# Another fixed task list for a one-core kernel of chunked attention with memory and a SiLU feed-forward block

## The chip, the cores and the metric

The kernel runs on one core of one Trainium2 chip. The core has five engines that run side by side, each with its own instruction stream that it takes in order: TensorE (PE, matrix products; its weight loads are PEld), VectorE (DVE), ScalarE (ACT), GpSimd (POOL) and SyncE (SP, here only the issuer of DMAs). The metric is the device time of one run in microseconds. Before the change it is 305.55 us, the median of 3 runs (305.26 to 305.59).

## The reference

Input x has 2048 tokens of 640 features in bf16. There are 32 heads of 20 features, and the sequence is cut into 4 segments of 512 tokens. Cut to what matters:

```python
h  = x + A(layernorm(x))          # attention with memory
h2 = h + B(layernorm(h))          # B(y) = silu(y @ w1) @ w2, w1 is 640 x 1728

# A: q, k, v = x @ wq, x @ wk, x @ wv, per head and segment s
logits = q_s k_s^T * 20**-0.5 + causal mask
a_dot  = softmax(logits) @ v_s
a_mem  = phi(q_s) @ M / (phi(q_s) @ z + 1e-6)   # phi(t) = t+1 if t > 0 else exp(t)
o_s    = g * a_mem + (1 - g) * a_dot            # g = sigmoid(beta), per head
M += phi(k_s)^T @ v_s ;  z += sum over phi(k_s) # for the next segment
A = concat(o_s) @ wo
```

## The kernel before

Everything is cut into about 1490 **tasks**, each a few instructions on one engine, and a list written out in the code, `ORDER`, fixes their order. `Graph.schedule` walks the list: the name gives the task, what follows a slash gives its engine where it has a choice (A for ACT, D for DVE), and the numbers after a colon give the buffer slots it takes in its pools. `Tracker` then records reads and writes of every buffer slot and puts semaphore waits before the instructions that need them. So the list decides three things: the order on each engine, the engine of each task that can run on two, and the slots. In time the engines run freely against each other, held only by these waits. PSUM has eight banks of 512 f32 columns (pool `ps`), and a score task takes four of them.

The tasks, with the line that issues them in the kernel before. The first digit of a name is the segment:

- `x0` to `x12`, `w_...`, `beta`: loads (L567, L570, L579). x0, x1 and the weights go out on SP, x2 and x3 on ACT's queue. x4, x8 and x12 bring four blocks of 128 tokens each, the first four one block each.
- `zpad` (L583): a zeroed tile on DVE. `warm` (L585): an activation on ACT that reads it. `fillN` (L604): N matmuls of zpad by zpad, 256 columns each, into a free bank; nobody reads the result. `sel` (L618) builds an identity on DVE from POOL's `iota`.
- `n1_st`, `n1_ra`, `n1_rb`, `n1_ap` (L711 to L732): layer norm of a block: statistics on DVE, reciprocal root in two steps on POOL, application on DVE. For the first four blocks `n1_tp` (L741) transposes on PE against the identity and `n1_te` (L750) copies the result to xT on ACT. Later blocks go through `n1_tr`, a transposing DMA on SP (L756). `n2_...` is the same for the second layer norm, with hT as its target.
- `re_wq`, `re_wk` (L682 on ACT, L684 on DVE): wq and wk copied into a layout by groups of four heads.
- `v`, `ve` (L783, L793/L794): v of a block, and its copy to Vx. `pr`, `qe` (L817, L825/L826): one group column of q or k, and its copy to QK. `ex`, `pha`, `phb` (L832, L839, L845): phi of it. `vt` (L857): twelve small DMAs per segment on SP, which put the rest of q and k, features of the last 12 heads, into tile QKV.
- `qk` (L893), `e` (L904), `mk` (L915): scores of four heads into four banks, two exponentials on ACT of two banks each (1024 or 768 elements per partition) into tile PT, and the causal mask on POOL. Segment 0 is cut in two halves (x and y); from segment 1 on a group has parts a, b and a shared part e.
- `av`, `oe`, `tn`, `nm`, `ad` (L936, L949/L951, L965 and L969, L982 to L1002, L1010): PT times V, copy, transposition back to tokens together with the memory's part, division, and addition into otok.
- `kt`, `mz`, `ma`, `mb` (L1050 to L1094): the memory: a transposing DMA of phi(k), products with V, accumulation, masking with constants that `mt`, `mta`, `mtb`, `mm` and `mzc` (L643 to L657) build once on POOL.
- `ot`, `wo`, `rs` (L1111, L1119, L1127): transposing DMA, output projection, residual.
- `h1`, `th`, `s` (L1148/L1153, L1162, L1168): feed-forward: product with w1, tanh on ACT, and (tanh + 1) times the product on DVE into sT. Two buffers hold the tanh. In segment 0 each runs in two halves of 256 columns.
- `h2`, `o`, `out` (L1195, L1208, L1213): product of sT with w2 in four parts, residual, store. The last block is stored in three column parts.

Segments overlap: while segment s has its scores and exponentials, the list places the projections of segment s+1 and the feed-forward block of segment s-1 between them on PE.

Of the kernel before, what the change touches and what calls it, by code (L numbers as in the profile page):

```python
# [373 lines left out]
mk6x_256 w_w1_1 w_w1_4 ve10/D qk2ya0:4 mk7x_0 v13:0 e2ya2:5 n1_ra9 mk7x_256 mk1yb_256 e2ya0 tn0y:2 av7x:3 ve13/D n1_rb8
oe7x/A:0 qk2yb0:4 nm0y:1 tn7x:0 e2yb0:1 av6x:1 nm7x:2 tn5x:2 av1y:3 e2yb2 oe6x/D:1 nm5x:3 tn6x:0 oe1y/A:0 qk3ya0:4
mk2yb_0 nm6x:0 e3ya0:2 n1_rb10 ot1:0 mk2yb_256 pha011:0 phb011 e3ya2 tn1y:2 pr101:1 mz02:0 qe101/D:0 av2y:3 ot0 ma02/A:3
qk3yb0:4 oe2y/D:1 mz00:1 e3yb2:0 phb041 pr100:3 ma00/D:0 kt01:1 nm1y:1 e3yb0 tn2y:2 zf1 qe100/D qk4ya0:4 mk3yb_0 kt04:0
wo1:0 e4ya0:6 nm2y:2 mk3yb_256 mtb1 e4ya2 w_w2_2 av3y:3 rs1 w_w1_3 ex031:0 qk4yb0:4 oe3y/D:0 w_w1_2 wo0:0 e4yb2:5
n2_st1:5 w_w2_1 e4yb0 epsg1 tn3y:2 ex101:1 n2_ra1 rs0 mm5 qk5ya0:4 pr140:3 n2_rb1 mk4yb_0 n2_st0:2 e5ya2:0 e5ya0 pr121:0
n2_ap1:0 n2_ra0 nm3y:0 qe140/A:0 mt0 n2_rb0 n2_tr1:0 qk5yb0:4 pr141:1 mta0 e5yb2:3 n2_ap0:2 mk4yb_256 n2_tr0 e5yb0 mtb0  # L380
pha031:1 phb031 av4y:2 mm6 qk6ya0:4 mm4 qe121/D:0 ex140:2 mk5yb_0 pr111:3 e6ya2:6 mk5yb_256 e6ya0 pr120:0 qe111/D:0
qe141/D ex121:0 qk6yb0:4 pha101:2 av5y:3 e6yb0:4 oe4y/D:0 h1_0_7_0:1 qe120/D e6yb2 h1_0_0_0:2 oe5y/D:1 th0_7_0:1 mk6yb_0
mk6yb_256 qk7ya0:4 th0_0_0:0 s0_7_0:0 tn4y:0 h1_0_8_0:3 e7ya0:2 nm4y:3 mz01:1 s0_0_0 mz04:0 e7ya2 ma01/D:2 phb101 kt10:0
kt03:1 h1_0_3_0:2 ma04/D:1 tn5y:1 th0_8_0:1 qk7yb0:4 th0_3_0:0 s0_8_0 av6y:0 e7yb0:0 s0_3_0 h1_0_1_0:3 nm5y:1 e7yb2
h1_0_12_0:2 th0_1_0:1 mk7yb_0 qk8a0:4 th0_12_0:0 pr110:1 e8a2:1 s0_12_0 s0_1_0 mm0 mk7yb_256 e8a0 mzc0 h1_0_10_0:2
qe110/D av7y:3 th0_10_0:1 vt19:0 qk8e0:4 s0_10_0 pr130:1 e8e2:0 vt16 oe6y/D:1 w_w2_3 n1_ap10:2 oe7y/D:0 e8e0 h1_0_5_0:2
pha121:0 qe130/D:0 w_w2_0 h1_0_11_0:3 th0_5_0:1 mk8e_0 qk8b0:4 s0_5_0 th0_11_0:0 tn7y:0 h1_0_6_0:1 e8b0:6 nm7y:3 mz03:2
ma03/D:4 s0_11_0 e8b2 h1_0_2_0:0 pha100:0 n1_ap8:1 h1_0_13_0:2 pha120:0 th0_2_0:1 qk9a0:4 mk8b_0 th0_13_0:0 pr131:3
s0_13_0 e9a2:4 mk8a_0 s0_2_0 mk8b_384 e9a0 h1_0_4_0:0 qe131/D n1_tr8:0 mk8e_256 h1_0_9_0:2 pha141:2 th0_6_0:1 mm3
th0_4_0:0 qk9b0:4 s0_6_0 mzc4 mzc6 ex100:1 mk9a_0 vt17 av8:3 s0_4_0 th0_9_0:1 mzc3 pha110:0 e9b2:3 h2_0_0:0 mm2 phb100  # L390
phb121 s0_9_0 mm9 pha111:1 mtb2 vt18 vt110 mzc9 mm8 e9b0 mm11 h2_0_1 oe8/D:0 mzc5 n1_tr10 ex141:1 mk9b_0 mm10 qk10a0:4
tn6y:3 h2_0_2 e10a2:5 phb141 mm1 vt11 nm6y:0 mzc2 n1_rb9 h2_0_3 e10a0 vt13 mb01:0 mm7 vt111 mzc1 qk10b0:4 mk9b_384 o0
h2_1_0:2 e10b2:2 ot3 mb00:0 e10b0 tn8:0 h2_1_1 n1_tr11 ex120:0 mk10b_0 nm8:2,1 qk10e0:4 ex111:1 h2_1_2 vt15 mk10b_384
phb111 n1_ap9:0 e10e2:1 mk10a_0 vt14 av9:0 e10e0 phb120 ot2 h2_1_3 oe9/A:0 ex110:0 mk10e_0 mk10e_256 qk11a0:4 kt12:1 o1
wo3:0 e11a0:6 pha130:0 mb02:0 phb110 e11a2 vt10 av10:2 rs3 n1_tr9 ex131:0 qk11b0:4 mk11a_0 oe10/D:1 tn9:0 e11b0:2
nm9:1,0 vt12 wo2:2 e11b2 ex130:1 mk11b_0 qk12a0:4 rs2 v20:0 e12a2:4 n2_st2:7 mzc7 e12a0 mzc8 mk11b_384 av11:2 pha131:0
n2_st3:1 ve20/A:1 qk13a0:4 mz12:3 e13a0:2 e13a2 v21:0 ma12 kt11:1 n2_ra3 phb130 n2_rb3 mzc11 mz10:3 n2_ra2 mzc10 ve21/A
n2_rb2 qk12b0:4 ma10 n2_ap3:1 ad8:0 e12b0:6 tn10:0 n2_tr3 pr210:3 nm10:0,1 mk13a_0 e12b2 mb03:0 qe210/A:0 ad9 qk12e0:4
oe11/D:1 pr220:0 e12e0:0 phb131 mk12b_0 n2_ap2:2 kt13:0 e12e2 mk12b_384 pr231:1 pha140:0 mk12a_0 qe220/A:0 n2_tr2
mk12e_0 qk13b0:4 qe231/D:0 tn11:2 e13b2:5 pr200:0 mk12e_256 nm11:3,0 ad10 e13b0 av12:1 qe200/D:0 mk13b_0 qk14a0:4 v23:2  # L400
e14a2:1 phb140 mk13b_384 oe12/D:1 mb04:0 e14a0 av13:1 ve23/A qk14b0:4 mz13:0 e14b2:3 pr221:2 ma13 oe13/D:0 e14b0
h1_0_7_1:3 qe221/A mk14b_0 qk14e0:4 th0_7_1:1 tn13:0 s0_7_1 mk14a_0 pr211:2 nm13:3,1 mk14b_384 e14e0:0 e14e2 h1_0_8_1:3
qe211/D mk14e_0 qk15a0:4 th0_8_1:1 pr241:0 e15a0:4 s0_8_1 mk14e_256 ad11 e15a2 av14:2 qe241/D:0 ad13 mz11:1 oe14/A:0
qk15b0:4 ma11 mk15a_0 e15b0:1 tn14:2 h1_0_4_1:1 nm14:3,1 e15b2 pr201:0 th0_4_1:1 mk15b_0 tn12:4 s0_4_1 qe201/A
h1_0_12_1:7 nm12:0,0 mk15b_384 qk16b0:0 e16b0:2 th0_12_1:0 ad14 av15:6 h1_0_13_1:4 ad12 oe15/D:0 e16b2 pr240:5 pha200:0
s0_12_1 th0_13_1:1 pha210:0 pha211:0 tn15:6 s0_13_1 qe240/A ex210:0 qk16a0:0 nm15:0,0 pr230:4 e16a2:6 e16a0 h1_0_10_1:5
qe230/D ad15 h1_0_6_1:6 phb210 th0_10_1:1 mb10:0 ot6:0 qk16e0:0 th0_6_1:0 s0_10_1 h1_0_0_1:7 ex211:0 mk16b_0 s0_6_1
v22:4 e16e2:5 mk16b_384 ot7 th0_0_1:1 e16e0 s0_0_1 h1_0_5_1:6 vt210:0 h1_0_11_1:7 ve22/A mk16e_0 mk16a_0 ot4 qk17b0:0
th0_5_1:1 wo6:4 mk16e_256 e17b2:3 s0_5_1 phb211 out1 e17b0 ot5 av16:6 rs6 ex220:2 qk18b0:0 pha220:0 th0_11_1:0 wo7:4
vt23 kt21:0 phb220 e18b2:0 oe16/D:1 e18b0 s0_11_1 h1_0_9_1:6 rs7 h1_0_3_1:7 th0_9_1:1 n2_st6:6 ex221:1 qk17a0:0 vt21  # L410
wo4:4 th0_3_1:0 e17a0:6 s0_9_1 n2_ra6 kt14:1 mk17b_0 s0_3_1 e17a2 h1_0_1_1:6 rs4 vt28 vt22 h1_0_2_1:7 mb12:0 mk17b_384
th0_1_1:1 n2_st7:4 n2_rb6 qk18e0:0 vt211 th0_2_1:0 wo5:4 e18e2:1 s0_2_1 vt26 n2_ra7 mk17a_0 s0_1_1 e18e0 vt24 mb13:0
av17:6 rs5 n2_rb7 ex231:2 vt27 vt29 qk18a0:0 pha231:0 mk18e_0 ex200:0 n2_st5:0 vt20 e18a2:5 n2_st4:3 n2_ap7:0 h2_2_0:4
# [855 lines left out]
```

## Time and profile before

| | us |
|---|---|
| median of 3 runs | 305.55 |
| span of the profiled execution, first to last instruction | 303.6 |
| own time of that execution | not given beside its span; the median is 1.95 above the span |
| TensorE clock granted over the span | 1.00 |
| PE, chain of work that ended last | 72% of the span |
| ACT, same chain | 12% |
| DVE, same chain | 7% |
| exponentials (L904) on ACT | 156.3 busy, x168 |
| causal masks (L915) on POOL | 81.5 busy, x128 |
| h2 (L1195) and h1 (L1153) on PE | 64.8 and 62.5 busy |
| fillers (L604) on PE | 9.1 busy, x61 |

The profile is of one execution. An engine's busy time counts an instruction from its start to its end, also where it has to wait for something on the way; matmuls overlap, so the mean duration of one (about 300 ns for 320 columns) is longer than the spacing at which they follow each other. The chain of work that ended last is followed back from the last instruction, at each step to what released it. A stage table gives the busy time of every engine in a stretch of the span.

### The profile page before, as it was taken

What the parts mean: (1) busy time and instruction counts of PE and PEld (TensorE: products, weight loads), DVE (VectorE), ACT (ScalarE), POOL (GpSimd) and SP (SyncE); (2) the same over time, 40 slices, a digit from 0 to 9 for tenths busy, and PEclk for the clock granted to TensorE, in tenths of its full rate; (3) what the DMA queues carried; (4) which work ended last, traced back from release to release, by engine and by line L of the source; (5) the groups of instructions that cost most, each with busy time, mean ns of one, the idle gap of its engine ahead of it and who ended that gap; (6) DMA issues with size and microseconds to landing.
All of it is one profiled execution on the core that took longest, in us unless ns stands there. A gap on an engine that the chain in (4) does not pass through costs nothing.

```text
span 303.6 us, 7334 instructions
## 1 busy us (share of the span) xinstructions
PE 294.4 (97%) x2934; PEld 167.9 (55%) x2934; DVE 214.4 (71%) x492; ACT 226.6 (75%) x321; POOL 141.7 (47%) x280
## 2 busy tenths in 40 slices
...
GB/s 211 363 104 159 69 153 87 272 37 77 166 87 75 39 42 2 2 122 69 106 154 42 67 19 0 2 89 69 56 97 36 2 0 89 43 66 66 0 3 107
DMA packets 48721, 24.65 MB, mean 81 GB/s; under 512 B 39152, under 2 KB 47600, under 8 KB 48688
## 3 DMA queue, kind: packets, MB, share of 16 engines
...
q10 hardware_dynamic: 288, 0.33, 0.4%
...
## 4 chain that ended last, share of the span: by engine, by line
PE 72%; ACT 12%; DVE 7%; DMA 4%; SPq 2%; issue 1%; POOL 0%; ACTq 0%
PE ps_all L1195 17%; PE ps_all L1153 13%; PE ps_all L817 13%; ACT PT L904 8%; PE ps_all L893 7%; PE ps_all L1119 6%; PE ps_all L783 5%; PE ps_all L936 5%; DVE sT L1168 3%; DMA wv_sb<-in_A_wv_dram 2%; ACT th L1162 2%; PE ps_all L965 2%; PE ps_all L1058 2%; DMA x_tok<-in_A_x_dram 1%; PE ps_all L969 1%
## 5 line engine op out<-in xcount | busy, mean ns | idle before, releaser
L904 ACT ACTIVATE PT<-ps_all 128x1024 bf16<-128x1024 f32 (+1 forms) x168 | 156.3, 985 | 16.9 <-PE ps_all L893 15.9
L915 POOL TENSOR_SCALAR_AFFINE_SELECT PT<-PT 128x512 bf16<-128x512 bf16 x128 | 81.5, 650 | 52.8 <-ACT PT L904 51.5
L1195 PE MATMUL ps_all<-w_sb,sT 128*128 128x320 bf16 (+2 forms) x462 | 64.8, 295 | 0.1
L1153 PE MATMUL ps_all<-hT,w_sb 128*128 128x512 bf16 (+1 forms) x325 | 62.5, 337 | 0.5 <-DVE sT L1168 0.4
L1162 ACT ACTIVATE th<-ps_all 128x512 f32<-128x512 f32 (+2 forms) x70 | 34.0, 505 | 35.1 <-PE ps_all L1153 24.6
L1168 DVE SCALAR_TENSOR_TENSOR sT<-th,ps_all 128x512 bf16<-128x512 f32 (+2 forms) x70 | 37.6, 558 | 23.8 <-ACT th L1162 23.2
L1195 PEld LDWEIGHTS ps_all<-w_sb,sT 128*128 128x128 bf16 x462 | 43.2, 98 | 18.5 <-issue 1.9
L1153 PEld LDWEIGHTS ps_all<-hT,w_sb 128*128 128x128 bf16 x325 | 29.8, 98 | 25.4 <-issue 2.1
L1010 POOL TENSOR_TENSOR otok<-on 128x320 bf16<-128x320 bf16 x24 | 19.2, 804 | 23.7 <-DVE on L1002 23.6
L711 DVE BATCH_NORM_STATS2 stt<-x_tok 128x6 f32<-128x320 bf16 x64 | 27.8, 476 | 3.4 <-DMA x_tok<-in_A_x_dram 3.2
L1208 DVE SCALAR_TENSOR_TENSOR x_tok<-ps_all,x_tok 128x640 bf16<-128x640 f32 (+3 forms) x18 | 13.3, 748 | 19.0 <-PE ps_all L1195 18.9
L720 POOL TENSOR_TENSOR rst<-mvt,eps_c 128x1 f32<-128x1 f32 x32 | 7.1, 223 | 40.4 <-DVE mvt L714 36.0
L817 PE MATMUL ps_all<-xT,wqr 128*128 128x512 bf16 x100 | 25.0, 381 | 0.0
L783 PE MATMUL ps_all<-wv_sb,xT 128*128 128x320 bf16 x160 | 24.4, 300 | 0.4 <-DMA wv_sb<-in_A_wv_dram 0.3
L817 PE MATMUL ps_all<-xT,wkr 128*128 128x512 bf16 x100 | 24.8, 380 | 0.0
L1119 PE MATMUL ps_all<-wo_sb,oT 128*128 128x320 bf16 x160 | 24.1, 299 | 0.4 <-DVE rd L996 0.2
L936 PE MATMUL ps_all<-PT,Vx 128*32 128x256 bf16 (+3 forms) x576 | 24.4, 287 | 0.0
L893 PE MATMUL ps_all<-QK 20*128 20x256 bf16 (+3 forms) x360 | 20.5, 286 | 1.0 <-ACT PT L904 0.7
L1002 DVE TENSOR_TENSOR on<-ps_all,rd 128x640 bf16<-128x640 f32 x24 | 19.8, 824 | 1.9 <-POOL otok L1010 1.1
L826 DVE CAST QK<-ps_all 128x512 bf16<-128x512 f32 x25 | 16.9, 684 | 5.1 <-PE ps_all L817 5.0
L1119 PEld LDWEIGHTS ps_all<-wo_sb,oT 128*128 128x128 bf16 x160 | 14.8, 97 | 8.1 <-issue 2.8
L783 PEld LDWEIGHTS ps_all<-wv_sb,xT 128*128 128x128 bf16 x160 | 14.7, 98 | 7.9 <-issue 1.5
...
## 6 DMA issues: line engine op xcount, KB each, us to landing
...
```

Of the source, the lines that this page charges most:

```text
L711: T.add(DV, lambda e, hh=hh: e.bn_stats(out=stt[:, s, 6 * hh:6 * hh + 6], in_=xb[:, 320 * hh:320 * hh + 320]), reads=R((xa, xsub)), writes ...
L783: fns.append(lambda e, c=c, hh=hh: e.matmul(bank(ps, hh)[:, 0:320], lhsT=xT[:, c, 128 * i:128 * i + 128], rhs=wv_sb[:, c, 320 * hh:320 * h ...
L817: fns = [lambda e, kc=kc: e.matmul(bank(ps)[:, lo:hi], lhsT=wt[:, kc, c, :], rhs=xT[:, kc, lo:hi], start=(kc == 0), stop=(kc == NC - 1)) f ...
L893: fns.append(lambda e, j=j, o=o, r=r, q0=q0, q1=q1, qa=qa, ka=ka: e.matmul(ps_all[:, o:o + q1 - q0], lhsT=ka[32 * r:32 * r + DH, 128 * j:1 ...
L904: T.add(AC, lambda e: e.activation(out=pt[:, pta.slot, q0:q0 + 2, 0:width], in_=sc3[:, b0:b0 + 2, 0:width], func=ACT.Exp, scale=SCALE), re ...
L915: T.add(PO, lambda e: e.affine_select(out=v, in_=v, pattern=[[0, 4], [1, 128]], compare_op=ALU.is_ge, fill=0.0, base=0, channel_multiplier ...
L936: fns.append(lambda e, j=j, r=r, h=h, pa=pa, pt=pt, co=co, q0=q0, ji=ji: e.matmul(bank(po)[32 * r:32 * r + 32, q0:hi], lhsT=Vx[:, vx.slot, ...
L1119: fns.append(lambda e, c=c, hh=hh: e.matmul(bank(ps, hh)[:, 0:320], lhsT=oT[:, c, 128 * i:128 * i + 128], rhs=wo_sb[:, c, 320 * hh:320 * h ...
L1153: fns = [lambda e, c=c: e.matmul(bank(ps)[:, lo:hi], lhsT=w1_sb[:, c, 128 * f:128 * f + 128], rhs=hT[:, c, lo:hi], start=(c == 0), stop=(c ...
L1162: T.add(AC, lambda e: e.activation(out=th[:, tha.slot, lo:hi], in_=bank(ps)[:, lo:hi], func=ACT.Tanh, scale=0.5), reads=R((ps, [0])), writ ...
L1168: T.add(DV, lambda e: e.scalar_tensor_tensor(out=sT[:, f, lo:hi], in0=th[:, tha.slot, lo:hi], scalar=1.0, in1=bank(ps)[:, lo:hi], op0=ALU. ...
L1195: fns.append(lambda e, f=f, t0=t0, fr=fr, hh=hh, n=n: e.matmul(bank(pa, hh)[:, 0:n], lhsT=sT[:, f, t0:t0 + 128], rhs=w2_sb[:, fr, c0 + 320 ...
```

## The change

The list `ORDER` is replaced by another list of the same tasks. No task is added or removed except fillers: before, fill30, fill8, fill7, fill6 and fill10 (61 matmuls); after, fill3, fill46 and fill23 (72). 25 tasks move from ACT to DVE and 15 from DVE to ACT; the loads keep their order up to `w_w1_0`, and the other loads of x8, w1 and w2 now follow directly on SP, ahead of the first `vt`. Slots change throughout. Apart from the list one line changes: for segments 1 to 3 the task `s` declares that it writes both halves of its sT column block, where it declared the first half only. Lines below the list move by two (L567 becomes L569, and so on). The list is cut to the rows that the text speaks of:

```diff
@@ ORDER, its first ten rows @@
-zpad:0 vpad0 iota x3:4 x1:3 x0:7 x2:5 sel w_wv:0 warm:0 vpad1 w_q:0 w_k halfc epsc beta x4:0,1,2,6 n1_st0:1 w_wo:0
-w_w2_4 n1_st1:6 n1_ra0 w_w1_0:0 n1_rb0 n1_ap0:0 n1_ra1 n1_st2:2 fill30:0 n1_tp0:4 n1_rb1 n1_te0/A:0 n1_st3:0 n1_ra2
-epsg0 n1_rb2 fill8:1 v00:0 mt1 n1_ap2:1 n1_ra3 n1_ap1:0 n1_rb3 n1_tp1:2 n1_tp2:6 mt2 n1_ap3:2 n1_te1/A re_wq1/D:0
-n1_tp3:4 n1_te2/A re_wq4/D v01:2 ve00/D:1 n1_te3/A re_wq2/A pr010:6 re_wk0/A:0 re_wk1/D ve01/D pr011:7 qe010/D:0
-re_wk3/D re_wk4/A lsc0 lsc1 re_wq0/D pr001:0 re_wk2/D qe011/A qk1x0:4 qe001/D:0 pr000:1 e1x2:5 n1_st6:0 e1x0 pr021:0
-re_wq3/D qe000/A n1_ra6 mk1x_0 lsc2 n1_st7:4 ex001:0 qk0x0:4 n1_rb6 pr020:2 e0x2:0 mt3 mk1x_256 qe021/D:0 e0x0 lsc3
-pr041:3 n1_st5:5 qe020/A vt00:0 n1_st4:7 qk2x0:4 n1_ra5 qe041/A:0 mk0x_0 pr031:1 zf0 vt09 vt06 e2x2:2 n1_rb5 mk0x_256
-pr030:0 e2x0 n1_ap5:2 pha041:1 x8:8,9,10,11 qe031/A:0 mk2x_0 vt03 qk0yb0:4 qe030/D av1x:3 e0yb0:1 pr040:2 mk2x_256
...
+mt3:0 iota mta3 vpad0 vpad1 halfc mt0 x1:3 sel x3:4 n1_st3:0 zpad mt1 mta0 x0:7 n1_st0:1 x2:5 epsg0 epsc n1_ra3 n1_rb3
+mtb0 n1_ap3:2 n1_ra0 n1_rb0 n1_st2:2 n1_ra2 n1_rb2 mm6 n1_st1:6 n1_ra1 n1_rb1 mtb3 n1_ap0:0 mm8 w_wv:0 w_q:0 w_k mm0
+n1_ap2:3 mt2 mta2 beta x4:0,1,2,6 w_wo:0 mm4 mtb2 mm7 warm:0 w_w2_4 w_w1_0:0 x8:8,9,10,11 n1_ap1:1 w_w1_1 mta1
+re_wq1/D:0 mm10 mtb1 mm5 mm3 re_wq3/D w_w2_1 re_wq0/D re_wq4/D w_w1_2 re_wq2/D re_wk3/D:0 re_wk0/D re_wk2/D n1_st5:5
+w_w1_4 n1_st6:0 n1_ra5 mm9 w_w2_2 n1_st7:4 w_w2_0 mm1 n1_rb5 mm11 fill3:0 n1_ra6 fill46:1 w_w2_3 w_w1_3 n1_tp3:6
+n1_te3/A:0 n1_ap5:2 n1_rb6 n1_ra7 n1_rb7 n1_st4:7 n1_ra4 n1_rb4 re_wk4/D w_w2_5 fill23:2 n1_tp0:6 n1_tp2:1 n1_tp1:3
+n1_te0/A n1_te2/A n1_te1/A zf0 zf1 mzc10 mzc7 mzc5 mzc1 mzc8 re_wk1/A lsc0 lsc1 mzc11 epsg1 n1_ap4:0 n1_st10:3 n1_ra10
+mzc9 mm2 mzc2 n1_rb10 n1_st9:1 n1_ra9 n1_rb9 n1_st11:2 n1_ra11 lsc2 n1_rb11 mzc0 mzc4 v00:6 n1_st8:6 n1_ra8 pr010:5
+qe010/A:0 mzc6 n1_rb8 lsc3 pr000:4 qe000/A:0 n1_ap9:3 mzc3 ve00/A:1 v01:0 ve01/A pr011:5 qe011/A ex011:0 pr001:2
+n1_ap10:1 pha011:0 phb011 qk1x0:3 e1x2:5 qe001/A e1x0 mk1x_0 mk1x_256 pha001:1 pr020:7 qe020/A:0 pr021:5 qe021/A
...
@@ ORDER, rows with the other fillers of before @@
-e3x0 ex021:2 ve02/D vt05 vt010 qk4x0:4 mk3x_0 n1_ra4 tn0x:2 e4x0:6 nm0x:0 vt01 mk3x_256 e4x2 n1_st8:6 fill7:3 qk0ya0:0
-mta1 vt02 av3x:4 e0ya0:5 mk4x_0 vt08 oe3x/D:1 n1_st10:0 mk4x_256 e0ya2 fill6:5 qk1ya0:4 n1_tr6 v11:0 n1_rb4 e1ya0:0
-n1_st11:3 n1_ra10 mta3 kt00:1 n1_ra8 e1ya2 av4x:2 ve11/D:0 tn2x:3 n1_ra11 phb021 qk5x0:4 n1_ap4:3 fill10:0 v12:0 e5x2:2
...
@@ ORDER, its last rows @@
-s3_0_0:0 h1_3_1_0:4 h1_3_7_0:0 th3_1_0:1 th3_4_0:0 h1_3_6_0:2 s3_4_0 o10 th3_5_0:0 h1_3_3_0:5 s3_5_0 h1_3_2_0:7
-h1_3_8_0:1 th3_7_0:0 s3_7_0 s3_1_0 th3_3_0:1 h1_3_9_0:3 th3_6_0:0 s3_3_0 h1_3_10_0:4 s3_6_0 th3_9_0:1 s3_9_0 h1_3_12_0:5
-th3_10_0:1 th3_2_0:0 h1_3_13_0:6 s3_2_0 h1_3_11_0:0 s3_10_0 th3_12_0:0 h2_14_0:2 s3_12_0 th3_13_0:0 th3_11_0:1
-h2_15_0_0:7 h2_13_0:4 s3_11_0 s3_13_0 th3_8_0:1 h2_15_1_0 s3_8_0 h2_13_1 h2_15_2_0 h2_15_0_1:6 h2_15_3_0 h2_12_0:0
-h2_13_2 h2_13_3 h2_12_1 o13 out13 h2_12_2 h2_12_3 h2_14_1 o12 o15_0 out15_0 h2_14_2 out12 out10 h2_14_3 h2_15_1_1 o14
-h2_15_2_1 h2_15_0_2:7 h2_15_3_1 out14 o15_1 out15_1 h2_15_1_2 h2_15_2_2 h2_15_3_2 o15_2 out15_2
...
+n2_tr14 h2_10_0:0 h2_10_1 h2_10_2 h2_10_3 o10 n2_tr13 h2_8_3 o8 out8 out10 h2_9_0:4 h2_9_1 h2_9_2 h2_9_3 o9 out9
+h1_3_8_0:0 th3_8_0:1 s3_8_0:0 h1_3_13_0:6 th3_13_0:0 s3_13_0 h1_3_3_0:3 th3_3_0:1 h1_3_4_0:1 th3_4_0:0 s3_3_0 s3_4_0
+h1_3_6_0:7 h1_3_12_0:0 h1_3_2_0:6 th3_12_0:0 s3_12_0 th3_6_0:1 s3_6_0 th3_2_0:0 s3_2_0 h1_3_7_0:1 th3_7_0:0 s3_7_0
+h1_3_0_0:4 th3_0_0:0 s3_0_0 h1_3_1_0:6 h1_3_5_0:7 th3_5_0:1 th3_1_0:0 s3_1_0 s3_5_0 h1_3_11_0:1 th3_11_0:1 h1_3_10_0:2
+s3_11_0 h1_3_9_0:0 th3_9_0:0 s3_9_0 th3_10_0:1 s3_10_0 h2_14_0:6 h2_14_1 h2_14_2 h2_14_3 h2_15_0_1:5 h2_15_1_1
+h2_15_2_1 h2_15_3_1 o15_1 out15_1 h2_15_0_0:4 h2_15_1_0 o14 out14 h2_13_0:0 h2_13_1 h2_13_2 h2_13_3 o13 h2_12_0:2
+h2_12_1 h2_12_2 h2_12_3 out13 h2_15_2_0 o12 out12 h2_15_3_0 o15_0 out15_0 h2_15_0_2:5 h2_15_1_2 h2_15_2_2 h2_15_3_2
+o15_2 out15_2
...
@@ the task s, in declare_back @@
-                        op0=ALU.add, op1=ALU.mult), reads=R((ps, [0]), (tha, [0])), writes=R((sa, [(f, q)])))
+                        op0=ALU.add, op1=ALU.mult), reads=R((ps, [0]), (tha, [0])), writes=R((sa, [(f, q)] if s == 0 else [(f, 0), (f, 1)])))
```

On each engine the new list begins so: DVE with sel, n1_st3, zpad, n1_st0, n1_ap3, n1_st2, n1_st1, n1_ap0, n1_ap2, n1_ap1 and then seven rearrangements; PE with fill3, fill46, n1_tp3, fill23, n1_tp0, n1_tp2, n1_tp1, v00, pr010, pr000, v01, pr011, pr001 and qk1x0; ACT with the loads x3 and x2, warm, n1_te3, n1_te0, n1_te2, n1_te1, zf0, re_wk1, lsc0, qe010, qe000, ve00, ve01, qe011, ex011 and e1x2; SP, after the loads, with vt09, vt00, vt03, n1_tr5, nine more vt, n1_tr6, kt02, n1_tr4, kt00 and n1_tr7.

165 lines of the change are left out of this document (83 added, 82 removed).

## The prediction

> **What bounds the kernel now.** I read the page's busy shares and 40 slices first, then the stages, the timeline of the first 20 us, the waits, and the single instructions of the trace. Each engine runs its instructions in the order of the list, so the trace gives every task's start and end.
>
> From the page, and from the table by stage (columns: stage, its length, then busy us and count on PE, weight load, DVE, ACT, POOL):
>
> ```profile
> PE 294.4 (97%) x2934; PEld 167.9 (55%) x2934; DVE 214.4 (71%) x492; ACT 226.6 (75%) x321; POOL 141.7 (47%) x280
> ```
>
> ```profile
> 0.00:10.00 10.00, 7.33 (x51) 5.38 (x52) 5.96 (x17) 3.25 (x3) 4.78 (x21) 1.00 0.76 247
> ...
> 80.00:100.00 20.00, 19.76 (x227) 11.45 (x225) 15.30 (x35) 19.04 (x26) 12.89 (x33) 1.00 0.42 74
> ...
> 240.00:260.00 20.00, 20.00 (x182) 12.48 (x181) 12.59 (x24) 7.79 (x13) 6.16 (x10) 1.00 0.25 34
> ```
>
> PE is over 90% busy from 10 us to the end. ACT is 87 to 97% busy from 20 to 200 us; after 240 us it is nearly free and PE alone decides. A busy PE may still be waiting, so I took, for each kind of task, the spacing from its first matmul to the next task's first, and its lower quartile (v and wo 1.36 us, pr 1.09, h1 of 512 columns 1.08, a full h2 row block 3.81, a score task 0.33). These quartiles add up to 273.6 us without fillers. From v00 at 9.03 to the last matmul at 301.07 are 292.0 us, for 276.1 us of quartiles and mid-kernel fillers: PE waits some 16 us in all, spread over hundreds of pieces. So the kernel is a start, then PE work nearly end to end, and what a new order can win is small unless it moves the start.
>
> The start, from the timeline:
>
> ```profile
> 1.12 5.03 PE L604 MATMUL ps_all<-zpad 128*128 128x256 bf16 x30 [1.12 <-DVE zpad L583]
> ...
> 4.78 0.89 DVE L711 BATCH_NORM_STATS2 stt<-x_tok 128x6 f32<-128x320 bf16 x2 [2.41 <-DMA x_tok<-in_A_x_dram]
> 5.71 0.21 DVE L714 BATCH_NORM_AGGREGATE mvt<-stt 128x2 f32<-128x12 f32 x1
> ...
> 7.36 0.45 PE L741 MATMUL ps_all<-ident,xn_rot 128*128 128x128 bf16 x5 [1.20 <-DVE xn_rot L732]
> 7.65 1.04 PE L604 MATMUL ps_all<-zpad 128*128 128x256 bf16 x8
> 7.85 0.70 ACT L750 ACTIVATE xT<-ps_all 128x640 bf16<-128x640 f32 x1 [3.58 <-PE ps_all L741]
> 9.03 1.52 PE L783 MATMUL ps_all<-wv_sb,xT 128*128 128x320 bf16 x10 [0.35 <-DMA wv_sb<-in_A_wv_dram]
> ```
>
> The 30 fillers need only zpad, which DVE writes first, so they lie wholly in the wait for x. Singly, the first 15 stand 213 ns apart and the others 109 ns. v00 waits for wv, which lands at 8.9.
>
> **The change, part by part.**
>
> *Start on PE.* The new list puts zpad on DVE behind sel and n1_st3. x3 is the first block to land: its load is issued at 0.80 and lands 3.0 us later, so st3 runs from 3.8, and zpad, which comes after its 1.05 us, is written by 5.0. PE's first work is now 49 fillers (fill3 and fill46), from 5.05: 15 x 0.2135 + 34 x 0.109 = 6.9, to 11.95. Then n1_tp3 (5 x 0.056 = 0.28), then 23 more fillers (2.5) to 14.75, then tp0, tp2, tp1. The first tp took 0.45 to its end and te0 0.70 after 0.04, so te0 ends at 15.95 and v00 starts at **16.0 instead of 9.03: +7.0**. None of that is hidden: in the old start PE had done v00 and v01 and begun pr010 by 13.0. Nothing else is late in the new order: the four ap are done by about 10 us (st and ap at 1.05 and 0.45 each from 3.8), wv lies there at 8.9, wq lands at 11.1 and its five rearrangements, now all on DVE, end by 13.1. It is the fillers that hold PE.
>
> The Trainium skill, "TensorE: Matmul & The Clock Gate", Part 1, says that the half-rate phase is a free-running window of about 3.4 us, not a number of matmuls, and gives 6, 11 and 14 half-rate matmuls for one kernel. The trace agrees in kind (15 at 213 ns, 3.2 us); no run here yet shows the spread. By 6 of them at half rate the 49 fillers would take 6.0 us, and v00 would start 0.9 us earlier.
>
> *What comes off PE later.* The old list has 7 + 6 + 10 fillers between 30 and 38 us; the new one has none there: -23 x 0.109 = **-2.5**. The tp1 to tp3 that followed v00 now lie before it: -3 x 0.28 = **-0.85**. If the old fillers only sat in waits that remain, the 2.5 comes back; if the waits go too, it is won. I take it as won, since 5.9 us of work leaves ACT (below), and keep 0 as the other end.
>
> *PE order from there.* I added the quartiles ahead of each landmark in both lists. What is left is the same to 0.1 us at v10, wo0, qk8a0, h2_0_0, v20, v30 and h1_2_4_0, and within 2.5 us at the other landmarks from qk0ya0 to wo12; only the last wo and h1 tasks change places by more. So beyond 70 us the list is a local shuffle, which removes no PE work: its gain can only come out of waits. In the last 60 us (from qk31a0) the old order takes 60.6 us for 60.4 us of work, so nothing is to be had there; the new order of the last h1 tasks keeps 1.9 us of h2_14 between the last of them and the first part that needs it (th 0.60 + s 0.68), so nothing is lost either.
>
> *ACT.* Tasks change engine: 25 go from ACT to DVE (9 qe, 9 oe, 3 ve, 3 rearrangements, 1 Mz copy), 15 the other way. By quartiles ACT goes from 218.2 to 212.3 us, DVE from 207.9 to 213.2, still about 72%. Following the new list by the rows: pr010 17.4, pr000 18.5, v01 19.6, pr011 21.0, pr001 22.0, qk1x0 23.1, first exponential (e1x2) at **23.5 instead of 16.72**, with 200.7 us of ACT work left instead of 207.9. Until e16a0 (127.31 in the old trace) the old ACT has 99.2 us of work in 110.6, the new one 96.3; at the same 11.4 us over the quartiles it gets there at 131.2, **3.9 late**. PE's sum, 7.0 - 2.5 - 0.85, gives **3.6 late**. Both agree.
>
> *What the shuffle may win.* 6.7 us of ACT's 11.4 are gaps over 0.12 us between 16.7 and 130 us. Five of the seven that last half a microsecond or more lie where two score tasks on shared banks follow each other with no other ACT task between: the second score waits for the first's exponentials. The waits show both sides (us in total, times, longest):
>
> ```profile
> ACT PT L904 <- PE ps_all L893: 15.9, 30, 1.2
> ...
> PEld ps_all L893 <- ACT PT L904: 13.3, 43, 0.8
> ```
>
> Up to e16 the old list has five such neighbours and the new one five too (0ya-1ya, 5x-6x, 4yb-5ya, 11a-11b, 11b-12a). So I give the shuffle little: **-1.0**, between 0 and all of the 6.7.
>
> *Loads, POOL, the sT edit.* Ten loads (x8 to x11, w1, w2; 4.6 MB) move ahead of the vt copies on SP; the old start moved 5.1 MB in 17 us, so they land by about 35 us. x8 comes first, at about 21 us, in time for st9 to st11 behind DVE's rearrangements. Price 0; a rival takes the other case. The early mask constants on POOL (it is busy 7.5 of the first 20 us, and its first mask came at 18.40) cost 0. The wider write of s1 to s3 waits for the h2 reads of the stage before; those stand ahead of the h1 on PE whose tanh s waits for anyway: 0.
>
> Sum: +7.0 - 2.5 - 0.85 - 1.0 = **+2.65**. The profiled execution spans 303.6, so the new span is 306.2. The page gives no time of its own for that execution; the median of the runs, 305.55, is 1.95 above the span, and I carry this over as what lies around it: **308.2 us**. Ends: all ACT gaps won, 3.65 - 6.7 = -3.1, so 302.4; fillers' waits return and nothing is won, 7.0 - 0.85 = +6.15, so 311.7.
>
> **Rivals.**
>
> 1. *The lighter ACT pays for the start (faster).* From e1x2 to e12b0 the old ACT needed 8.6 us above its quartiles, 5.0 of them gaps. Without gaps the new one reaches e12b0 at 23.5 + 75.2 + 3.6 = 102.3, against 101.94: only 0.4 late. From there PE has 192 us of work for which it took 199.6; if half of those 7.5 us of waits go, 0.4 - 3.75 = -3.35: **302.2**. It decides from the point where over 3.65 us of waits are gone. For it: 5.9 us less on ACT. Against: the equal count of neighbours, and 16 us of waits in pieces of about 0.1 us.
> 2. *SP becomes late (slower still).* tr6, tr4 and tr7 now stand behind nine vt copies. The last eight cannot start before qe030, about 32.7 by my walk, and took 5.64 us on SP before; with two kt of 1.28 between the transposes, tr4 lands at about 43.6 and tr7 at 46.2. PE can reach v10 at 42.9 and v13 at 44.6. Stall 0 to 2 us; where the copies also queue behind the loads, 2: **310.2**. For it: beta's 8 KB took 9.4 us behind the big loads.
> 3. *Nothing to measure.* The recovery happens to be 3.65: **305.5**.
>
> **Chances.** Forecast 0.46, SP late 0.17, ACT pays 0.28, nothing 0.09. A measurement of this kernel tells about 0.2% (0.6 us) from no change. Slower 0.63, same 0.09, faster 0.28. The range runs from rival 1's 302.2, just under the lower end above, to the upper end, 311.7.
>
> **What would show it.** v00 at 16.0 with 49 and 23 fillers ahead of it, the first 15 at 213 ns; e1x2 near 23.5; no filler after that; qk8a0 at 72 to 75 (69.44 before); e16a0 at 128 to 131; the last 60 us unchanged in length. Wrong if v00 starts before 14, if PE's waits after it sum to under 12 us (16 before), or if v10 and v13 wait for a DMA.

## The result and the profile after

The changed kernel takes **314.09 us** (median of 4 runs, 313.22 to 315.07) against 305.4 (4 runs, 305.19 to 305.59): ratio 1.0285, 95% interval 1.0258 to 1.0313. It is 8.7 us slower; the forecast was 308.2, with a range of 302.2 to 311.7. The profiled execution took 314.17 with a span of 312.4 at a granted clock of 1.00. Three executions far off all others, two of e7 (1610 and 481 us) and one of the kernel before (1610 us), are left out of the ratios and counts below.

The page's busy shares after:

```profile
PE 296.3 (95%) x2945; PEld 169.4 (54%) x2945; DVE 221.7 (71%) x505; ACT 221.4 (71%) x308; POOL 143.8 (46%) x280
```

ACT has lost 5.2 us (forecast 5.9) and DVE gained 7.3 (5.3), and PE has hardly more to do. The start, from the timeline of DVE and PE:

```profile
3.78 0.89 DVE L713 BATCH_NORM_STATS2 stt<-x_tok 128x6 f32<-128x320 bf16 x2 [2.21 <-DMA x_tok<-in_A_x_dram]
...
4.88 0.17 DVE L585 MEMSET zpad<- 128x128 uint32 x1
```

```profile
5.11 8.41 PE L606 MATMUL ps_all<-zpad 128*128 128x256 bf16 x49 [5.11 <-DVE zpad L585]
13.35 0.44 PE L743 MATMUL ps_all<-ident,xn_rot 128*128 128x128 bf16 x5
13.63 2.67 PE L606 MATMUL ps_all<-zpad 128*128 128x256 bf16 x23
16.14 1.00 PE L743 MATMUL ps_all<-ident,xn_rot 128*128 128x128 bf16 x15
17.38 1.53 PE L785 MATMUL ps_all<-wv_sb,xT 128*128 128x320 bf16 x10 [0.24 <-ACT xT L752]
```

zpad comes behind n1_st3 and the fillers hold PE, as the prediction walked it. But 28 of them stand at 213 ns (5.11 to 11.05), not 15, so v00 starts at 17.38 and not at 16.0. The stages (columns as before):

```profile
30.00:40.00 10.00, 8.31 (x99) 3.77 (x97) 4.18 (x11) 10.00 (x16) 6.02 (x10) 1.00 0.35 62
...
80.00:100.00 20.00, 19.59 (x198) 12.28 (x199) 13.21 (x33) 19.42 (x31) 8.66 (x14) 1.00 0.39 71
240.00:260.00 20.00, 20.00 (x198) 9.92 (x197) 14.00 (x26) 14.55 (x22) 8.13 (x12) 1.00 0.01 2
```

and the two sides of the scores in the waits, which were 15.9 and 13.3 us:

```profile
ACT PT L906 <- PE ps_all L895: 17.9, 30, 1.5
...
PEld ps_all L895 <- ACT PT L906: 13.9, 41, 0.9
```

The lighter ACT has not opened the middle: from 80 to 100 us it is still 97% busy, and it waits more, not less. I call a task's start minus its start in the trace of before its **lag**. It is +8.35 at v00, +8.20 at e1x2, +7.05 at v03 (33.7 us), +7.05 at v13 (50.0), +7.25 at qk16a0 (133), +8.56 at v30 (176), +8.86 at the last h2 task. So most of the loss is made before 18 us; 1.3 us of it comes back by v03, and 1.8 us is added behind v13.

### The profile page after: what moved, and what is told of

Same layout as the page of the kernel before. It is cut to its first block, busy times and chain, and to the rows that moved or that the text cites. A ratio compares the mean times of both kernels' runs of the same rounds, so it can differ in the third digit from the quotient of the medians.

```text
span 312.4 us, 7365 instructions
## 1 busy us (share of the span) xinstructions
PE 296.3 (95%) x2945; PEld 169.4 (54%) x2945; DVE 221.7 (71%) x505; ACT 221.4 (71%) x308; POOL 143.8 (46%) x280
## 4 chain that ended last, share of the span: by engine, by line
PE 72%; ACT 13%; DVE 9%; DMA 4%; issue 2%; POOL 0%; ACTq 0%
PE ps_all L1197 20%; PE ps_all L1155 13%; PE ps_all L819 10%; ACT PT L906 9%; PE ps_all L895 6%; PE ps_all L785 5%; PE ps_all L1121 5%; PE ps_all L938 4%; PE ps_all L606 3%; PE ps_all L967 2%; ACT th L1164 2%; PE ps_all L971 1%; DMA oT<-otok 1%; DVE stt L713 1%; DMA phiKt<-phiK 1%
## 5 line engine op out<-in xcount | busy, mean ns | idle before, releaser
L906 ACT ACTIVATE PT<-ps_all 128x1024 bf16<-128x1024 f32 (+1 forms) x168 | 156.9, 992 | 18.6 <-PE ps_all L895 17.9
L917 POOL TENSOR_SCALAR_AFFINE_SELECT PT<-PT 128x512 bf16<-128x512 bf16 x128 | 82.8, 651 | 71.9 <-ACT PT L906 68.4
L1210 DVE SCALAR_TENSOR_TENSOR x_tok<-ps_all,x_tok 128x640 bf16<-128x640 f32 (+3 forms) x18 | 13.3, 747 | 22.3 <-PE ps_all L1197 22.2
L953 DVE TENSOR_SCALAR oTs<-ps_all,lsc 128x512 bf16<-128x512 f32 (+1 forms) x28 | 17.3, 619 | 4.3 <-PE ps_all L938 3.9
L1121 PEld LDWEIGHTS ps_all<-wo_sb,oT 128*128 128x128 bf16 x160 | 14.8, 98 | 9.1 <-issue 2.2
## 6 DMA issues: line engine op xcount, KB each, us to landing
w_sb<-in_B_w_dram SPq DMA_DIRECT2D x5, 432.0 KB, 10.8
x_tok<-in_A_x_dram SPq DMA_DIRECT2D x3, 640.0 KB, 10.7
sT<-in_A_wk_dram SPq DMA_DIRECT2D x1, 800.0 KB, 10.8
```

The costliest lines, as they stand in the source:

```text
L906: T.add(AC, lambda e: e.activation(out=pt[:, pta.slot, q0:q0 + 2, 0:width], in_=sc3[:, b0:b0 + 2, 0:width], func=ACT.Exp, scale=SCALE), re ...
L917: T.add(PO, lambda e: e.affine_select(out=v, in_=v, pattern=[[0, 4], [1, 128]], compare_op=ALU.is_ge, fill=0.0, base=0, channel_multiplier ...
L1121: fns.append(lambda e, c=c, hh=hh: e.matmul(bank(ps, hh)[:, 0:320], lhsT=oT[:, c, 128 * i:128 * i + 128], rhs=wo_sb[:, c, 320 * hh:320 * h ...
```

## The experiments

All ratios are to the kernel before on the same chip, with 95% intervals. "Clock below 1" counts the executions whose granted clock over the span was under 0.996. Lags are from the profiled execution, which for e3 and e11 is 1.7 us under the median of the executions and for the others within 1.3 us of it. In the traces of e9 to e18, 24 or 25 matmul records are missing; their places are taken from the weight loads.

| kernel | us | ratio | clock below 1 | v00 at | lag v03 | v10 | qk16a0 | last h2 |
|---|---|---|---|---|---|---|---|---|
| after | 314.1 | 1.0285 [1.0258, 1.0313] | 1 of 4 | 17.4 | +7.0 | +7.3 | +7.3 | +8.9 |
| e1_zpad_first | 310.1 | 1.0160 [1.0137, 1.0184] | 3 of 4 | 12.1 | +1.8 | +3.5 | +4.2 | +5.6 |
| e2_short_start | 309.8 | 1.0154 [1.0122, 1.0186] | 3 of 4 | 10.3 | +0.5 | +4.4 | +2.8 | +5.0 |
| e3_no_fill | 311.6 | 1.0209 [1.0174, 1.0245] | 4 of 4 | 10.7 | +2.0 | +4.3 | +3.7 | +4.6 |
| e4_old_late | 312.1 | 1.0236 [1.0218, 1.0255] | 0 of 4 | 14.8 | +5.8 | +6.0 | +5.9 | +6.8 |
| e5_short_loads | 312.2 | 1.0240 [1.0204, 1.0275] | 4 of 6 | 10.4 | +1.5 | +4.1 | +4.5 | +6.8 |
| e6_loads_back | 316.5 | 1.0359 [1.0326, 1.0391] | 4 of 6 | 16.6 | +6.3 | +7.6 | +9.9 | +11.4 |
| e7_old_engines | 310.1 | 1.0162 [1.0148, 1.0176] | 0 of 4 | 8.8 | +0.7 | +0.8 | +2.7 | +4.8 |
| e8_old_nofillmid | 305.6 | 1.0016 [0.9998, 1.0034] | 4 of 12 | 8.3 | -0.5 | -1.4 | -1.4 | +0.2 |
| e9_short_old_engines | 340.7 | 1.1162 [1.1123, 1.1201] | 6 of 6 | 17.2 | +13.0 | +15.5 | +28.3 | +36.4 |
| e10_short_masks | 311.5 | 1.0233 [1.0203, 1.0262] | 6 of 6 | 10.6 | +0.8 | +4.0 | +3.4 | +5.9 |
| e11_short_both | 337.9 | 1.1085 [1.1043, 1.1126] | 6 of 6 | 15.9 | +7.5 | +10.3 | +22.8 | +30.8 |
| e12_late_old_engines | 339.9 | 1.1121 [1.1085, 1.1156] | 6 of 6 | 16.6 | +11.8 | +15.0 | +27.2 | +34.7 |
| e13_short_refilled | 312.8 | 1.0213 [1.0168, 1.0258] | 4 of 6 | 10.3 | -0.1 | +8.8 | +7.4 | +8.4 |
| e14_short_spread | 313.2 | 1.0239 [1.0206, 1.0271] | 5 of 6 | 10.2 | +0.8 | +6.8 | +7.2 | +9.2 |
| e15_old_tuned | 306.5 | 1.0035 [1.0019, 1.0052] | 7 of 12 | 9.1 | +0.0 | -0.8 | -1.2 | +1.1 |
| e16_spread_nofill | 313.4 | 1.0276 [1.0250, 1.0302] | 4 of 4 | 10.4 | +0.6 | +4.7 | +5.3 | +7.9 |
| e17_old_early_loads | 312.6 | 1.0241 [1.0214, 1.0268] | 4 of 4 | 8.9 | +0.9 | +7.5 | +7.5 | +7.0 |
| e18_free_slots | 310.9 | 1.0171 [1.0132, 1.0209] | 6 of 6 | 10.3 | +0.8 | +2.2 | +3.3 | +6.1 |

**Theory**: the late start is the loss and is carried one to one. **Rival**: the new order has a floor of its own behind it, in ACT, in DVE or on SP.

### The start alone

```diff
e1: new list, zpad first
-mt3:0 iota ... n1_st3:0 zpad mt1
+zpad:0 mt3 iota ... n1_st3:0 mt1
e2: e1 and fewer fillers
-fill3:0 ... fill46:1 ... fill23:2
+fill30:0 ... fill18:2
e3: new list, no filler at all
e4: old list
-fill30:0
+fill100:0
```

> The new list with zpad first on DVE, as in the old list; all 72 fillers stay. Fillers from 1.1: 15 at 213 ns and 34 at 109 ns end at 8.0, tp3, 23 more to 10.8, v00 at about 12.1 instead of 17.4. Theory carry (PE's order bounds everything behind the start, a late v00 reaches the end one to one): 314.1 - 5.3 = 308.8. Rival absorb (the middle of the new list is held by ACT, SP or the loads, and an earlier start only turns into waits): over 311.5.

> The new list with zpad first, 30 fillers instead of 49 before tp3 and 18 instead of 23 behind it, so that each ends as its xn is ready: v00 at about 10.4. Carry: 314.1 - 7.0 = 307.1. Absorb: over 310.5, PE waits after v00 over 23 us instead of 20.0.

> The new list without any filler; zpad stays late. v00 at about 10.4, but PE begins at half rate then: 3.2 to 6 us of half rate (as in the old and in the new trace) cost 1.6 to 3 us. Carry: 314.1 - 7.0 + 1.6 to 3 = 308.7 to 310.1. Absorb: over 311.5. If the fillers were needed for the rate later on, over 314.

> The old list with 100 fillers instead of 30 before tp0, nothing else: 15 x 0.2135 + 85 x 0.109 = 12.5, tp0 at 13.6, v00 at 14.9 instead of 9.03 (+5.8), the waits of tp and te behind v00 shorter by 0.4. Carry: 305.4 + 5.4 = 310.8. Absorb: under 308.

e4 settles the first half of the theory: v00 is 5.8 us late, the lag stays at +5.8 to +6.0 until qk16a0 (132 us), and the end is +6.8. A late start is lost whole in the old order. e3 has no filler ahead of v00 and starts it at 10.7 us, e1 has all 72 and starts it at 12.1: with zpad first or without fillers the start is nearly back. In the new order the other half fails: e1 starts v00 5.2 us earlier than after and ends only 3.3 earlier, e2 7.0 and 3.8. So an early start takes off about half of the loss (4.0 and 4.3 us by the medians), and the rest stays. A part of that rest is the clock: the profiled e2 was at 0.994, while its one execution at 1.0 took 308.6 us, 5.4 less than the median of after at 1.0. e2 is level with the old list at v03 (+0.5) and has lost 4.0 us more by v10; 1.1 of these are a stretch at half rate on v12 (last section). So there is a second floor between 27 and 45 us, which the late start hides.

### Loads, engines and fillers, one at a time

```diff
e5, e6: nine w1 and w2 loads back to their old places in e2 and in after
-x8:8,9,10,11 n1_ap1:1 w_w1_1 ... w_w2_1 ... w_w2_5
+... n1_tr7 w_w2_5 w_w1_1 w_w1_4 ... kt04 w_w2_2 w_w1_3 w_w1_2 w_w2_1 ... vt19 w_w2_3 w_w2_0
e7: old order, the new list's 40 engine choices
-ve00/D:1 ... re_wq2/A ... qe010/D:0 re_wk3/D re_wk4/A
+ve00/A:1 ... re_wq2/D ... qe010/A:0 re_wk3/D re_wk4/D
e8: old list
-fill7:3 ... fill6:5 ... fill10:0
```

> The new list with the short start of e2_short_start (ratio to the old list 1.0154, some 4.7 us) and, besides, nine of the ten early loads (w1, w2) put back on SP to where the old list has them; x8 stays early, since DVE needs it. Theory two floors (a late start hides a second floor at 25 to 45 us, made by the loads ahead of vt and tr): the waits of v12, v10 and qk5x0 for a DMA (1.9 us) go, 304.9 + 4.7 - 1.9 to 2.5 = 307.1 to 307.7, ratio 1.007 to 1.009. If the floor is the list's own (POOL, ACT, score order): ratio stays at 1.013 to 1.016.

> The new list as it is, late start and all, with only the nine loads put back. Two floors: PE behind the late start did not wait for vt or tr, so ratio 1.026 to 1.029 (312.9 to 313.8). If the loads alone made the loss (the rival that SP becomes late): ratio under 1.02.

> The old list in its order, with the 40 engine choices of the new list alone: 5.9 us of work go from ACT to DVE. If PE's order paces the kernel: 1.000 +- 0.003. If ACT paces the stretch from 20 to 100 us: 2 to 4 us faster, ratio 0.987 to 0.993. If DVE's copies come later than ACT's did: slower by 1 to 2 us.

> The old list without fill7, fill6 and fill10 (23 matmuls between 30 and 38 us). If they lie in waits that remain: 1.000 +- 0.002. If they cost PE time, as the forecast had it: 2.5 us faster, ratio 0.992. If they keep the rate up: slower.

- e5, e6: the early loads do not make the floor (qk6ya0: +3.2 in e5, +3.5 in e2). Put back behind the late start (e6), they cost 2.4 us more. The loss is made at 70 us. SP issues, in e6 (a row runs from the start of its first DMA to the end of its last):

```profile
61.67 2.06 SPq L571 DMA_DIRECT2D w_sb<-in_B_w_dram  x4
65.05 7.95 SPq L757 DMA_TRANSPOSE hT<-xn_rot  x2
```

  and in after, where no load stands ahead of the same two transposes of hT:

```profile
64.86 4.54 SPq L758 DMA_TRANSPOSE hT<-xn_rot  x2
```

  Each of these transposes holds SP for 1.2 us; in e6 there are 5.5 us between the two. The first comes behind the four loads, DVE waits 3.3 us for the buffer that it reads before it can normalise the next block, and oe4y stands behind that on DVE: PE waits 2.7 us for it.

- e7: taking 5.9 us from ACT and giving 5.3 to DVE **costs** 4.8 us in the old order, spread from 20 to 200 us.
- e8: 23 fillers gone and nothing won at the end. Of the 2.85 us that they took, 0.9 came off by v10 (lag -0.5 at v03, -1.4 at v10); PE's scores waited 2.7 us from 26 to 50 us instead of 1.5. The lead of 1.4 us held to qk16a0 and was gone at v30 (+0.2): between them PE waits 0.8 us for the transpose of oT, and 1.2 us (0.3 in before) for DVE, which has the statistics of x12 ahead of it. The load of x12 waits for the store of the block before; that store took 4.2 us (1.9 in before), so the load went out at 156.2, no earlier than in before (156.0).

### The engines belong to the order

```diff
e9: e2 with the old list's 40 engine choices
e10: e2, DVE's statistics of x8 to x11, their POOL steps and seven constants behind the first masks
-n1_st10:3 n1_ra10 ... v00:6 n1_st8:6 ... n1_rb8 ... mk1x_0 mk1x_256
+v00:6 ... mk1x_0 mk1x_256 ... ve02/D n1_st10:3 n1_st9:1 ... oe0x/D:1 n1_st8:6
e11: e10 with the old engines
e12: after with the old engines
```

> The short start (zpad first, 30 and 18 fillers) of the new list, with the engines of 40 evictions and softmax tasks as the old list had them. Short start alone: ratio 1.015, last feed-forward block +5.04 us against the kernel before, v30 +4.63, qk6ya0 +3.48. Theory (the engine choices that spare ScalarE and load VectorE cost time gradually, as they did in the old list, +4.8): the lag at qk6ya0 falls little (to about +3), since that stall is GpSimd's and VectorE's, but the growth from qk16a0 (+2.8) to the end (+5.0) goes; end +2 to +3, ratio 1.006 to 1.010. Rival (the engines suit the new order and cost only in the old one): end +5 or more, ratio 1.015 or above.

> The short start of the new list, with the statistics of x8 to x11 (VectorE, 4 x 1.1 us at 22.6 to 26.8 us), their GpSimd pairs and seven constants moved behind the masks of the first windows. Theory (second floor of the start: the masks mk1x stand behind rows that wait for x8, 28.5 us instead of 18.4): the masks run from about 19.5 us, the wait v03 to av1x (1.58) goes, and of the +4.4 us at v10 about 2 go; end +3, ratio about 1.009. Rival (that wait only hides the next one, ScalarE or the transposes of x being as late): v10 still +4 and end +5, ratio 1.015.

> Short start, masks moved and old engines together. If both theories hold, the lag at v10 is about +2 and little is added after it: end +1 to +2, ratio 1.002 to 1.007. If the order itself (which task stands where from 60 us on) is the loss, the end stays at +4 or more, ratio 1.012 or above.

> The changed kernel as it is (zpad behind the statistics, all 72 fillers) with the 40 engine choices of the old list. Theory (the engines cost time by themselves): the lag stays +8.3 at v00 and about +7 at v10, and shrinks or stays from there instead of growing to +8.9; end about +6 to +7, ratio 1.020 to 1.024 instead of 1.0285. Rival (ScalarE, laden again, is the later one): end +9 or more, ratio 1.029 or above.

After e7 I held the engine choices for dear in themselves. e12 refutes it: put back, they cost another 26 us. e9 and e11 do the same with the short start, by 31 and 26 us over e2 and e10. The first piece is seen at 20 us, in PE's waits of e12:

```profile
PE ps_all L818 <- DVE QK L827: 4.0, 1, 4.0
```

pr011 waits for qe010. In after it runs on ACT at 20.03; in e12 it is on DVE, whose queue has the statistics of x4 to x11 ahead of it, and runs at 24.93. An engine choice is good only for the place in the order that it was made for, in both directions.

e10 took away the wait that it aimed at (qk4x0: +1.24 instead of +2.23), and another took its place at 33 us: the statistics, now ahead of oe2x, kept tn2x waiting 1.7 us. By v10 the lag was +4.0, not the +2.4 or so of the theory.

### Fillers and statistics in the gaps

```diff
e13: e2 with fillers in PE's gaps
+fill11:0 av1x:0 ... fill5:6 qk0ya0:3 ... fill5:6 av0x:0 ... fill4:6 v11:5 ... fill4:5 qk5x0:2 ... fill9:4 v12:0
e14: e2, statistics of x8 to x11 in DVE's gaps (behind oe1x, n1_ap7, nm3x, oe0y), 18 fillers
e15: e8 with three DVE tasks moved
-pha120:0 ... s0_2_0 ... n1_st12:0 h1_1_12_0:2 n1_st14:6 ... th1_12_0:0 s1_1_0 ... s1_12_0
+s0_2_0 pha120:0 ... s1_1_0 n1_st12:0 h1_1_12_0:2 ... th1_12_0:0 s1_12_0 n1_st14:6
```

> The short start of the new list with 38 fillers laid into TensorE's gaps at 27 to 40 us (11 ahead of av1x, 5 ahead of qk0ya0, 5 of av0x, 4 of v11, 4 of qk5x0, 9 ahead of v12). Theory (idle gaps bring a half-rate stretch of 2.1 us, in which ten matmuls of v12 take 267 instead of 136 ns, +1.1 to +1.4): no half-rate stretch after 6 us, v10 at about +3.2 instead of +4.4, end about +4, ratio about 1.011. Rival (the waits end last anyway, the half rate lies in them): v10 still +4.2 or more, ratio 1.015 or above.

> The short start of the new list with the statistics of x8 to x11 laid where VectorE stood idle (one behind oe1x, the others behind n1_ap7, nm3x and oe0y), their GpSimd pairs and constants behind the masks, and 18 fillers in the gaps that are left (ahead of qk0ya0, av0x, v11 and qk5x0). Theory (the middle's floor is VectorE's and GpSimd's queue position of the early statistics, 4.3 us of VectorE between 22.6 and 26.8, plus the half rate): v10 at +1 to +2, end +2 to +3, ratio 1.004 to 1.009. Rival (ScalarE's exponentials or the transposes of x hold it, whatever VectorE does): v10 at +3.5 or more, ratio 1.012 or above.

> The old list without its 23 middle fillers, with three moves on VectorE: s1_1_0 and s1_12_0 ahead of the statistics of x12 and x14 that wait for their load, and pha120 behind s0_2_0. Theory (the old list's late start is carried one to one, and what eats a gain is single places where a task stands behind another that waits): the wait h1_1_7_0 to mz23 (1.4 us) and half a microsecond at 77 us go, end about 1.5 us earlier than in that list without the moves, ratio 0.994 to 0.999. Rival (the wait is set by x12's load or by ScalarE): unchanged, ratio 1.000 to 1.002.

e13 and e14 missed their forecasts and tell nothing of the floor: their fillers take a bank that the exponentials of qk0ya0 still read, and PE stands 2 us at the filler itself (PE on ACT's PT, 3.3 and 2.1 us). e15 moved its two waits and got others of the same size behind them: at either clock slower than e8 (305.9 against 304.8 at 1.0).

### SP and the buffers of layer norm

```diff
e16: e14 without fillers
e17: old list, x8 and the nine loads early
-w_w1_0:0 n1_rb0
+w_w1_0:0 x8:8,9,10,11 w_w1_1 w_w2_1 w_w1_2 w_w1_4 w_w2_2 w_w2_0 w_w2_3 w_w1_3 w_w2_5 n1_rb0
e18: e16, x6 and x7 normalised early into slots of their own, transposes first on SP
-... n1_ap6:2 n1_tr6 ... kt02:0 ... n1_tr4 kt00:1 ... n1_ap7:2 n1_tr7
+n1_ap4:0 n1_ap6:1 n1_ap7:3 ... vt05 n1_tr6 ... vt04 n1_tr4 n1_tr7 ... kt02:0 kt00:1 w_w2_2 w_w2_0 w_w2_3 w_w1_3 w_w2_5
```

> The short start of the new list with the statistics of x8 to x11 in VectorE's idle time and their GpSimd pairs and constants behind the masks, no fillers after v00. Theory (queue places of the early statistics hold the middle): neither the wait v03 to av1x (1.58 in the short start) nor that at tn2x (1.77 with only the masks moved) is there, v10 at +1.5 to +2.5 instead of +4.4, end +3, ratio 1.007 to 1.010 with the granted clock at 1.0. Rival (ScalarE, Vx and the transposes hold it): v10 +3.5 or more, ratio 1.014 or above.

> The old list with x8 and the nine feed-forward weight loads moved to where the new list has them (behind w1_0). Theory (early loads cost nothing, the queue being free there, and the old order has hardly a wait on a transpose to win back): ratio 0.998 to 1.002. Rival (they delay the transposes vt0 and tr4 to tr6 behind them): v10 later by 1 us or more, ratio 1.003 or above; other rival (they free the queue at 45 to 80 us): end earlier by 0.7 us or more, ratio below 0.998.

> e16 (short start, early statistics of x8 to x11 spread, no fillers after v00) with x6 and x7 normalised at 22 us into buffers of their own (x8 to x10 take theirs behind v13), their transposes ahead of the last copies and of the two key transposes on SP, and five of the nine early loads moved to 40 us. Theory (transposes of x on SP and the one buffer behind them are the floor of 30 to 47 us): v12 has no wait for its transpose, v10 at +1 to +2.5 against the kernel before instead of +4.4, end +3 to +4, ratio 1.008 to 1.012. Rival (the exponentials and VectorE's evictions hold it): v10 stays at +3.5 or more, ratio 1.016 or above.

e16 missed too: v10 came at +4.7 instead of +1.5 to +2.5. e17 is the surprise: the loads that I had costed at 0 cost the **old** order 7.5 us by v10. SP, by start and length, in the old list:

```profile
25.84 1.30 SPq L756 DMA_TRANSPOSE xT<-xn_rot  x1
27.25 5.64 SPq L857 DMA_DIRECT2D QKV<-QK  x8
32.99 1.21 SPq L756 DMA_TRANSPOSE xT<-xn_rot  x1
...
36.27 2.52 SPq L756 DMA_TRANSPOSE xT<-xn_rot  x2
```

and in e17:

```profile
12.41 13.84 SPq L571 DMA_DIRECT2D w_sb<-in_B_w_dram  x9
26.36 3.22 SPq L858 DMA_DIRECT2D QKV<-QK  x4
29.68 1.37 SPq L757 DMA_TRANSPOSE xT<-xn_rot  x1
31.16 8.68 SPq L858 DMA_DIRECT2D QKV<-QK  x8
39.94 1.22 SPq L757 DMA_TRANSPOSE xT<-xn_rot  x1
...
42.51 2.60 SPq L757 DMA_TRANSPOSE xT<-xn_rot  x2
```

Nine loads hold SP for 13.8 us, everything behind them is late, and the transposes of x come at 39.9 and 42.5 instead of 33.0 and 36.3. (3.0 us of that are one copy, at 32.7, that holds SP for 3.7 us instead of 0.7; why is not shown.) PE waits 2.6 us for xT at v11 and 3.0 us at qk5x0, the first score that reads QKV, whose copies SP issues until 39.8 (the trace does not name what qk5x0 waits for); half rate from 41.7 to 45.4 adds about 1.5. The new order with a short start lies between the two; e2:

```profile
25.09 2.47 SPq L858 DMA_DIRECT2D QKV<-QK  x3
27.69 1.31 SPq L757 DMA_TRANSPOSE xT<-xn_rot  x1
29.05 7.95 SPq L858 DMA_DIRECT2D QKV<-QK  x9
37.10 1.22 SPq L757 DMA_TRANSPOSE xT<-xn_rot  x1
38.36 1.27 SPq L1051 DMA_TRANSPOSE phiKt<-phiK  x1
39.67 1.28 SPq L757 DMA_TRANSPOSE xT<-xn_rot  x1
40.99 1.27 SPq L1051 DMA_TRANSPOSE phiKt<-phiK  x1
42.30 1.27 SPq L757 DMA_TRANSPOSE xT<-xn_rot  x1
```

tr6, tr4 and tr7 stand behind nine copies and two transposes of phi(k), and n1_ap6 and n1_ap7 wait for the buffer that tr5 and tr6 read (n1_ap6 at 35.5 in e2; 27.6 in the old list). e18 undoes both, and issues five of the loads later besides:

```profile
28.00 2.98 SPq L858 DMA_DIRECT2D QKV<-QK  x4
31.49 1.21 SPq L757 DMA_TRANSPOSE xT<-xn_rot  x1
32.74 3.46 SPq L858 DMA_DIRECT2D QKV<-QK  x5
36.25 2.53 SPq L757 DMA_TRANSPOSE xT<-xn_rot  x2
```

PE no longer waits for xT, and the lag at v10 is +2.2, against +4.4 in e2 and +4.7 in e16, as the theory had it. But v10 is a poor place to compare. In e2 the half rate falls on v12, ahead of v10; in e18 it falls on v10 itself (43.5 to 45.4 us), about 1.1 us each. One task on, at v13, e18 has +3.4, e2 +4.2 and e5 +3.9, and at qk16a0 e18 (+3.3) is no better than e2 (+2.8). Nor had PE a wait for xT in e5 or e16. So the transposes of x, by SP's queue and the shared buffer, are one part of the floor in the middle, 0.8 us at v13 against e2; they are not the floor. PE's waits in e2 from 26 to 50 us show two parts of about the same size, and the half rate is a third:

```profile
PE ps_all L937 <- POOL PT L916: 1.4, 1, 1.4
PE ps_all L784 <- DMA xT<-xn_rot: 1.4, 2, 0.9
```

Whichever was taken away, others came: tn2x in e10 (1.7 us), the copies into QKV in e18 (1.2 us, 0.5 in e2). The time did not follow either (1.017, forecast 1.008 to 1.012). From qk16a0 on, the lag of e18 grows from +3.3 to +6.1. It grows in every kernel in the new order (after: +7.3 to +8.9; e2: +2.8 to +5.0), and also in the old order in e7 (+2.7 to +4.8), e8 (-1.4 to +0.2) and e15 (-1.2 to +1.1), so it is not a matter of the new order alone. Apart from the two places seen in e8 it is spread over waits of under 1 us, and its cause stays open. No version tried beats the kernel before.

## Why the prediction was wrong

By its own steps, with the lags of the profiled execution:

| step | forecast | measured |
|---|---|---|
| fillers behind zpad, v00 late | +7.0 | +8.35 |
| tp1 to tp3 moved ahead | -0.85 | -1.30 (v00 to v03, with a few shuffles) |
| mid-kernel fillers gone | -2.5 | 0.0 (v03 to v13) |
| shuffle and lighter ACT | -1.0 | +1.8 (v13 to the end) |
| sum | +2.65 | +8.86 |

- *Start on PE* was right in mechanism and short in size. Taking 15 matmuls at half rate from the old trace was the error: 13 more, at 213 instead of 109 ns, are 1.35 us, the whole difference. With the same 49 fillers e6 and e12 had 21 of them, and v00 at 16.6.
- *What comes off PE later* is the first step that failed in kind: "I take it as won", -2.5, and 0.0 came. PE's time above the quartiles from 20 to 60 us is 7.7 us in before, 2.85 of them fillers, and 7.9 in after without any. In the old order (e8) 0.9 of the 2.85 came off by v10 and later waits took that as well.
- *What the shuffle may win* failed by as much: -1.0 forecast, +1.8 measured. The lag grows by 1.6 from qk16a0 to the end; no run isolates why, so this cause stays open.
- *ACT*: the forecast gave the lighter ACT part of the credit. In e7 the same engine choices cost 4.8 us. By what path is not shown: the 22 copies out of PSUM that went to DVE there end 1.19 us after their product in the mean, against 1.12 on ACT, and only 11 of them later. In after, ACT's own waits for scores grew from 15.9 to 17.9 us. The check "both agree" said nothing for the 2.5: ACT's sum has no fillers in it. It has e1x2 6.8 us late and 2.9 us less work ahead of e16a0; measured are e1x2 8.2 late and e16a0 6.3, so 1.9 of the 2.9 came on ACT, while PE at qk16a0 was 7.25 late.
- *Loads at price 0* came out near 0 here: SP was done with them at 24.8, and behind the late start the first copy went out at 27.9. In the old order, with a start at 9 us, they go with a loss of 7.5 us by v10 (e17). In the new order with a short start they cost little: +4.4 at v10 with them (e2), +4.1 without (e5).
- Rival 1 (ACT pays) is refuted by e7 and by after's waits. Rival 2 (SP late) did not decide: v10 and v13 wait for no DMA in after. But its mechanism is real: it held the old order in e17, and in the new order it is one of the waits that the late start hid. The prediction treated it as an alternative to the late start; it lay behind it.
- The upper end of the range, 311.7, was "fillers' waits return and nothing is won". That came true, and with it 1.35 us from the half rate and 1.8 from the later growth, for which the range had nothing; the moved transposes gave 0.45 more than their 0.85. Of the signs named, the 49 and 23 fillers and the last 60 us (60.6 before, 60.2 after) came as said; qk8a0 (77.2) and e16a0 (133.6) came later than said.
